# Turning P with plain matmuls into two banks, as row tiles where that suits, in a new order of work

## The chip, the cores and the metric

The kernel runs on one core of one Trainium2 chip. The metric is the time of one execution on the device in microseconds. Before the change it is 1505.74 us, the median of three runs (1505.22 to 1508.84).

The core has a matrix engine (TensorE, PE in the profile, with its weight loads shown apart as PEld), three engines for elementwise work (VectorE is DVE, ScalarE is ACT, GpSimd is POOL) and a queue that issues transfers (SyncE, SP). TensorE writes to PSUM, which has eight banks; DVE and ACT copy results out of it to SBUF ("eviction").

## What is computed

A sequence of 2048 rows of 448 numbers goes through four layers, each adding to x: attention with a recurrent memory (A), a gated network (B), A again, B again, with one set of weights for both A and one for both B.

```python
for s in range(n_seg):                      # 64 segments of 32 rows
    h = jnp.concatenate([mem, xs], axis=1)  # 8 memory rows and 32 of x: 40 keys
    q, k, v = (jnp.einsum('btd,dhe->bhte', h, W) for W in (Wq, Wk, Wv))  # 16 heads of 256
    scores = jnp.einsum('bhqe,bhke->bhqk', q, k) * scale   # masked
    p = _softmax(scores, axis=-1)
    o = jnp.einsum('bhqk,bhke->bhqe', p, v)
    o = jnp.einsum('bhte,hed->btd', o, Wo)
    mem = o[:, :M, :].copy()                # the next segment's memory
    outs.append(o[:, M:, :])
# B: gate = x W_gate; gate * (gate > 0) * (x W_up), times W_down
```

(The three projections stand in one line here for brevity.) Each A and B works on the layer-normalised x. All arrays are bf16. The memory makes a recurrence: segment s needs the memory of segment s-1.

## The kernel before

**Algebra.** The weights are multiplied together at the start: A = Wq Wk^T per head, so that scores are h A h^T, and B = Wv Wo per head, so that the output is the sum over heads of (P h) B. P is the softmax of one head's scores, h the 40 rows of a segment.

**Two streams of work.** The recurrence is `chain`, one step per segment. Both A layers run in it at once, the second seven segments (`LAG`) behind the first, in 70 steps. Per step: U = mem A for all heads (line 936, 112 matmuls), evicted and rearranged; then `middle`: scores (L1130), softmax on DVE and ACT, the turn of P, Y = P h (`y_part`, L1187 and L1190), evicted to YTm; then O, the 56 products with B (L975), evicted as a high and a low part (Ohi, Olo); then these are brought into columns with the selector `Sel` (`cols`, L451), which gives the next step's memory mT. In many steps `middle` runs a second time, for rows of x of the second layer that ride along with the memory rows through U and O; there are 66 such calls, with tiles Pr and PTr in place of Pm and PTm.

The rest is streaming: `att_group` does the 32 rows of four segments for four heads (U at L1276, scores at L1302, softmax, the turn of Px, Y at L1187 and L1190, output at L451), 96 groups in all; `glu_units` (L1374) and `glu_down` do the B layers, `norm` the normalisation with its own transposes. The streaming work fills TensorE between the steps of the recurrence.

**The turn of P.** Y = P h needs P with keys on the partitions, so P is transposed on TensorE and evicted to PT. In `middle`, P is one tile of 128 rows (16 heads by 8 memory rows) by 128 columns (two segments of 64, of which 40 are used); the turn is one 128x128 transpose in bf16 into one bank, and one copy of 104 rows by 128 columns to PTm or PTr. In `att_group`, Px holds four segments; its turn is two transposes into one bank and one copy of 104 by 256 to PTx. That makes 136 turns of one transpose and 96 of two.

**Tilings.** TensorE works untiled (128x128), as two row tiles (64x128: L1276, L1187, L1190, L1374), as four column tiles (128x32: L975), as eight tiles (64x32: L936) or as two column tiles (128x64, at the start). An operation's `mode` says which.

**What sets the order.** Every operation is recorded with `add`, with what it reads and writes, its engines and a cost, and `_Sched` lays out all engines' queues at build time. TensorE's order is written out: LINE holds a character per TensorE operation, which says how far down the list of those left the next one stands. ORDER gives a shift of priority to each part of the streaming work, which sets the order on the other engines. For each copy out of PSUM the planner picks ACT or DVE by its costs, and for each result a bank of the pools C (two banks) and G (six). An operation may be given further tilings in `also`; `line` cuts TensorE's order into runs whose operations have a tiling in common, and gives the run the lowest such mode. Where the planner foresees a long wait of TensorE it puts in matmuls without a use (L1408, "warming matmuls" below). Each engine works through its queue strictly in order and waits on semaphores.

Of the kernel before, what the change touches and what calls it, by code (L numbers as in the profile page):

```python
# [13 lines left out]
H = 16  # L14
E_HEAD = 256
NPAIR = H // 2
M = 8
# [10 lines left out]
BF = dt.bfloat16  # L28
# [1 line left out]


STEPS = "ABCDEFGHIJKLMNOPQRSTUVWXYZabcdefghijklmnopqrstuvwxyz0"
ORDER = ("WaAPMPvTtHAmiKXsPbQwBZAAKVLahkUWfxoglheAggVZZIjCfbeJAXlzkAApmXXSQGGARFrGGMUgYLYEqpMcimntsnbaLdDaYNUaIKQasootaa"
         "IamHzatMbanGYaAKt0aaJQPfHNWZggWPXLeJgyAiS0Lu0paxXy0bJaaawJabqAwkXQsLnJ0P0xdYLuR0IrxJESoh0aprYvAKeakBaTde0apmfl"
         "0AxKjloNZCHdAbpsDsUzAeRDrSYQfCauramiRROdJWQSliYOAntmwDkLvpaU0ose0NVHbcTnnAxX00lknAmXoAEI0JXsWoNrWtaR0aBTzbAueA"
         "zxZcQ0q0gag0TH0DuL0awknFmlrwNUBkrnZMushahJaOgAABbmsGORqpMzXeAbTAdCgmAA0qpoI0a00TKDzwtajkhAYHgKXubMoLxaAcZMeAky"
         "UPvecasMa0GlwBpnnaDqvPuaft0lUJZwIPBAtdSRexIzd0gdp0TFG0ZVaWtamLdLF0tecZgoaFmCnSxLrSAKbVEWWUbAUcbZAQKUWznAD0DwFY"
         "LhfiQS0H0vSOAAXZbJUSsFaria0uvIkcEZwBqzeVgvNgOaALCXLR0bnstXIDN0xuLBcRcqpzdacfaiZlTMhk0gMMHRwaBkgAisGZYtMsUFn0zV"
         "IFNwJApRZfcAiutYgwLmYo0w0xvGkIAceuiXs0DasLaajayO0oeyil0F0AqRaRioYDVAtQYbmvOVuSte0WMUqA0yKPaKRav0IjNTTO0lKZJvdk"
         "PxyqdoWnhLpAGweRybtOxXTBtFxgRZFGuwtA0XA0luZtjAvlcgOC0JAfaBWaBpTiUEtfuUcpuev0O0plQOMQhQAShmmAGTYotfgpbleII0TaBM"  # L40
         "aPnZY0dxoBWpVcrAiqamnnNot0unVPyLvpKpqAsABVrANdQWsSSKlz0JcSfj0ElEpn0qPKwWzaAgaYo00Aa0Tlb0oupJCA0yVSxuTnA0zokfbp"
         "CrqRqZjtboAdaHNayVAlkpQAMirRvHYYjqcposgwBwuwNAPImgFcnygdasArDIapCO00J0IZchpGLumthtqLsYG0apAkaPAtIR0rAB0uPdaaaa"
         "aacpbuKLoaaaaaaaaaaaaaaaaaaaOmqe0NbraUgWsbrP")

SIGNS = "ABCDEFGHIJKLMNOPQRSTUVWXYZabcdefghijklmnopqrstuvwxyz0123456789+-*/=<>()[]{}.,:;!"
LINE = ("AFFFEIFLJHFEFEFEJJEFGFHEEAEDMHHEDDEDEDDLKHDGDFDDDDKAJ,CEDEDCCCCKJAEGCEDBBMBBIACEBDCAAJALAHEnAADCCFGDEBAdcAWAMA"
        "AWnBAETkCSBBAHANNAgMBAKBWCAHAHGBbDAUDCAYBHBAAADPAENREAFLQHABQFPPFAFBDACCCCFBBABAAAWAAAKARBAHOdAGSAZAQAAABMS~DB"
        "A~BggA(AeCAAbAa9AZZZDADCAETADDQQAAAAMAAKKKAJJAIHAHGABEBACABAAAABATMAXAKVcLKAMRX~JXAMLA~NAAAEEADGAaaFFCCABETBBR"
        "WACPAANNNOAALAMvLA0DJCIHHLGGGGAFHHAADEKAACBBAEAAAABAMBAYXQAJGaIIAQAVAAAGDDAODDdcAFBBDDAAUaAACRAQBBNNNNAALAALL3"
        "3JKArIOICHBGGGAFIHeAEAEAACBBFAAAABCAATMBAXWeAJUaKJhMAW]AcKKAAAKEEATDA76fGmF2CABF4yBxAAAuuuCBbsAEpRFponEAAAjBLB"  # L50
        "glQAe9eeeECHcbTcbSBYBuFWBAATAARAJDSOOOAAMANLNMBdAbJDIAAPGUGZBgYBeEEEFHAGQDAvuCD~LCCqADAnNrm~BDCkkkFAAhDD;hhAAA"
        "cdjDACCYAAAVaAUATTTA0TBRDQQBBANAAAKCJBAHHHAKHGBBSGGAdcDEAZALQCBKZJBXBBBUIcJIFFBADGA))CEEon/H)CAB9jA7KD5556AA3H"
        "A32Ahzhy4FAAvAulCsssAiBEEonBFmmlDDATNCflCWABbJJEYsYYYCYXKXAWWAAITAAAAPODVNbNNNAALLEJAK+9YYDD5AA9E2FA0DIyyyzAOH"
        "vAvvBRsRBxqADACCAAjDAhDCFieeeAAcDJAaaxCCAXAAVAZAnSSssWARRRBABANAAZAACBAAGYSdlSSHGhZAFRAVAMDYABBeKBBBxHYBJEEB)("
        "HGDACOG+CA=B7ADe4CAG1112bAAyAAxxwdDkAzsbBFgoEnEmmmneFAEiENihFf-DeAGchABa2IZZZBCXAYIVXWEATDARCAAOfTBNUBMMMPBLEA"
        "L98DXeDVGIA0FAQAwFDTt~JDssstAZApArqDnANDCjAiEAmAfCCdAcccEAAZAYAAAWWAAAaTSvnARsRABBANNNAAMLAAXdAAAqBTGdASFFhPYF"
        "AQAACSBBgMBBBbIBQEBI{]ACSCC<FECCA+LEA7gD5556AA3A44bAiz70AZAxAwvluuuvAcsGHqqqGGAFtmFFFjIiBEAEeeeINEeAaAcbFBkEYA"
        "GATaAASRDHPVDOOOAANMA//ACIJA8=OOVH4Nc26BA000BAPyDwAvvNCSCAqEBAnNClCoAjjjEAiAgOC4CeeAAAbCAYBBAVqyVAAASSSASoACAA"
        "AMAAKYAdtkCJVIATISAGZgAFAAACNARMBeLdBBBFQFBADA))FCEoE/CAN>BE8B7AnCC333AGA0A21EYEexvAAVtb;rriBBArnnnCDmlQAkkPCB"
        "NAmfAAAcAaaBZZZCAYXFXHWWIAGADRXAAPANNEMMMEMVVNLEJRA77Ife4AHA16B0BAyyyAfCAuAtvuAsKAJpDAtHmAlBBKiiiEAAfAeCBddEAA"  # L60
        "DCXAWAAUZAAmStSSSASogAAAOBibxAvAZAAjYXgAJeYViYJJBnAASGAAARDC1cCJAZIBBBzIyIBEJEEBD77GFAnCIC0AB4BxB~NwAXuuu~GDtA"
        "VAtsGFADoAPsAljAjiANMfffAAdNAAdcBQYZAOBJUBLSBWRrGQQQRSDIDNDGNMLAFaJCAAGOATAEYEEEIFAACAAxwCMCTsABDBHnsAmMCBjjjA"
        "JAhCfAgfC}BAcDAAZYBXAAVVVWAATAVUsrSTAYuBRAAOOAAMMMAAKAYeAtkBWJBAIHkRbRFGSBdBEUEDOAMCCCGGCFIC{]ItU,(ADAA/BA-NB9"
        "99+AKA6CA65CdBA81bAAA3x3BwvmuuuActtsGtsHGGzpGGGmGApkjISAAfffEDdOcIeee;DaHbDYDejYfPWWeWWWXAAUNBBcbB/xQQYAdDAVDM"
        "TCARRRAACRPOKQQDGLCAAKIAAHAFFAEEEAACCABAWOVJHMARXFBAUAHAAGFAAALCCPDCDCFAJJFEBBBBBAABAADAAAAABAAAAA")


class _Op:
# [363 lines left out]
def mm_cost(*ns):  # L432
    return sum(max(n, 54) / 2.4 + 2.5 for n in ns)
# [14 lines left out]
def packed(E, mode, out, lhsT, rhs, **k):  # L448

    if mode != 1:  # L450
        return E.matmul(out, lhsT=lhsT, rhs=rhs, **k)  # L451
    for j in range(4):
        q = slice(32 * j, 32 * j + 32)
        w = lhsT[:, q] if len(lhsT.shape) == 2 else lhsT[:, j // 2, 32 * (j % 2):32 * (j % 2) + 32]
        i = E.matmul(out[q], lhsT=w, rhs=rhs, tile_position=(0, 32 * j), **k)
    return i


# [53 lines left out]
class _Kernel:  # L512
# [604 lines left out]
    def middle(self, act, m, row, col, P):  # L1117

        s = self.s
        k_ = lambda n: (m["n"], n)  # L1120
# [29 lines left out]
        else:  # L1150
# [7 lines left out]
            for c, sg, l in act:  # L1158
                b = sg % 2
                s.add("dve", 238, lambda E, e, c=c, b=b: E.tensor_scalar(Pv[:, b, 0:L], m["E"][:, c, 0:L], m["st"][:, 4 + c:5 + c], None, op0=ALU.mult),  # L1160
                      r=[k_("Em"), k_("rc")], w=[k_(f"P{c}")], **P)
# [8 lines left out]
        def yy(E, e):  # L1170
# [6 lines left out]
        s.add("pe", mm_cost(*[128] * 3, 64, 64), yy, r=[k_("PT")] + [q for c, sg, l in act for q in self.hr_keys(l, sg)], w=yb, alloc=yb, mode=2, **P)  # L1177
# [72 lines left out]
    def att_group(self, l, t, g, bo):  # L1250
# [65 lines left out]
        bp = self.bank("G", "C")  # L1316
# [6 lines left out]
        s.add("pe", mm_cost(128, 128), pt, r=[("Px", si), "ident"], w=[bp], alloc=[bp], room=["PTx"])  # L1323
        s.add(EV, ev_cost(256, fast=True), copy_any(PT[0:104, :], lambda: bp.ap().bitcast(BF)[0:104, 0:256]), r=[bp], w=["PTx"])

        for p in range(2):
            HR = self.HR[l][b][p]
            s.part()
            yb = [self.bank("G", "C") for _ in range(2)]

            def yy(E, e, p=p, HR=HR, yb=yb):
                for q in range(5):
                    for h in range(2):
                        r0 = 64 * h
                        i = self.y_part(E, yb[h].ap(), HR, r0, q, PT[r0:r0 + L, 128 * p:128 * p + 128], 128)
                return i
            hk = [q for h in range(2) for q in self.hr_keys(l, 4 * t + 2 * p + h)]
            s.add("pe", mm_cost(*[128] * 3, 64, 64), yy, r=["PTx"] + hk, w=yb, alloc=yb, room=[("YT", yi, p, h) for h in range(2)], mode=2)
# [194 lines left out]
```

## Time and profile before

| | |
|---|---|
| median of three runs | 1505.74 us |
| the profiled execution's own time | 1504.3 us |
| its span, first to last instruction | 1501.8 us |
| PE, DVE, ACT, POOL busy | 1487.6, 1148.6, 908.3, 171.8 us |
| matmuls | 37,022 |
| granted TensorE clock | 1.0 of full |

In the profile a row of a group has line, engine, operation, the output and inputs by name, their shapes, and the count; then busy time and the mean duration in ns, then the engine's idle time just ahead and what ended it. A row of the timeline has start and length in us, and merges equal instructions (x16) that follow each other; the durations of TensorE's instructions overlap, since they include the way through the array. Shapes such as 64\*128 are the tile of TensorE that a matmul uses, 64 rows by 128 columns. The lines named L441 and L444 are the shared copy function on ACT and DVE, and L451 the function `packed`, which many untiled matmuls go through, so that tiles' names tell them apart.

### The profile page before, as it was taken

The page shows a single profiled execution, that of the slowest core. Times are in us where ns is not written, and L with a number is a line of the kernel's source. Part 1 is how long each engine was busy: PE and PEld are TensorE (multiplying, and loading weights), DVE is VectorE, ACT ScalarE, POOL GpSimd, SP SyncE. Part 2 cuts the span into 40 slices and gives each one's busy share as a digit, 9 for nine tenths or more (in the row PEclk, how much of TensorE's full clock was granted, in tenths as well). Part 3 has the DMA queues.
Part 4 walks back from the last instruction along what each step waited for, and adds up shares of the span by engine and source line. Part 5 has one row for each costly group of instructions (what it writes and reads, how often), then busy time and mean ns, then how long its engine had stood idle before and what let it go on. Part 6 is the DMA issues. An engine that isn't in the chain of part 4 may idle for free.

```text
span 1501.8 us, 83238 instructions
## 1 busy us (share of the span) xinstructions
PE 1487.6 (99%) x37022; PEld 1057.6 (70%) x37022; DVE 1148.6 (76%) x3561; ACT 908.3 (60%) x2519; POOL 171.8 (11%) x664
## 2 busy tenths in 40 slices
PE   9999999999999999999999999999999999999999
PEld 6557666667767776777768677677768776677776
DVE  6667678787778878687877877687777788787864
ACT  7776566666556666566655666466665556565643
POOL 3110111111111111011100111011100011010000
PEclk9999999999999999999999999999999999999999
DMA  7612100000000000000000000000000000000000
GB/s 228 186 31 65 50 11 8 12 9 8 8 4 16 8 8 14 4 18 6 16 5 11 12 8 15 4 17 6 18 4 8 13 9 14 5 11 5 12 8 11
DMA packets 62581, 34.11 MB, mean 23 GB/s; under 512 B 31872, under 2 KB 62096, under 8 KB 62224
## 3 DMA queue, kind: packets, MB, share of 16 engines
q1 hardware_dynamic: 62224, 28.80, 7.5%
q8 instruction: 291, 4.77, 1.3%
q14 instruction: 66, 0.54, 0.1%
HBM read 21.36 MB, written 1.84 MB: 15 GB/s over the span
## 4 chain that ended last, share of the span: by engine, by line
PE 95%; DVE 3%; ACT 1%; SPq 0%; issue 0%; DMA 0%; POOL 0%; DVEq 0%
PE psG L451 24%; PE psG L1276 17%; PE psG L1374 12%; PE psC L975 11%; PE psC L936 9%; PE psG L936 3%; PE psG L1187 3%; PE psG L763 3%; PE psG L1302 3%; PE psC L451 2%; PE psC L1187 1%; PE psC L1130 1%; PE psG L750 1%; PE psG L1190 1%; PE psC L1276 1%; PE psG L975 1%
## 5 line engine op out<-in xcount | busy, mean ns | idle before, releaser
L1276 PE MATMUL psG<-HT,A 64*128 64x128 bf16 x4968 | 285.7, 216 | 0.2
L451 PE MATMUL psG<-Bsb,YT 128*128 128x448 bf16 x1288 | 276.6, 352 | 0.0
L1276 PE MATMUL psG<-HX,A 64*128 64x128 bf16 x3726 | 266.9, 216 | 0.2 <-issue 0.2
L1276 PEld LDWEIGHTS psG<-HT,A 64*128 64x128 bf16 x4968 | 234.2, 94 | 13.7 <-issue 5.4
L441 ACT ACTIVATE Ug<-psG 64x128 bf16<-64x128 f32 (+2 forms) x428 | 153.6, 378 | 68.3 <-PE psG L1276 59.4
L1276 PEld LDWEIGHTS psG<-HX,A 64*128 64x128 bf16 x3726 | 194.0, 94 | 1.0 <-issue 0.8
L1374 PE MATMUL psG<-G,glu 64*128 64x128 bf16 x5936 | 187.9, 216 | 0.6 <-DVE G L444 0.2
L1374 PEld LDWEIGHTS psG<-G,glu 64*128 64x128 bf16 x5936 | 174.2, 94 | 12.8 <-issue 6.3
L975 PE MATMUL psC<-Bsb,YTm 128*32 128x448 bf16 x3584 | 181.4, 353 | 1.0 <-DVE YTm L444 0.6
L451 PEld LDWEIGHTS psG<-Bsb,YT 128*128 128x128 bf16 x1288 | 112.5, 97 | 89.3 <-issue 5.9
L936 PE MATMUL psC<-A,mT 64*32 64x448 bf16 x3948 | 154.7, 350 | 1.5 <-DVE Pr L1160 0.5
L1114 DVE STREAM_TRANSPOSE uT<-Usb 128x384 bf16<-128x384 bf16 x280 | 154.1, 551 | 0.9
L936 PE MATMUL psG<-A,mT 64*32 64x448 bf16 x3892 | 152.1, 350 | 0.0
L975 PEld LDWEIGHTS psC<-Bsb,YTm 128*32 128x32 bf16 x3584 | 89.9, 97 | 73.4 <-DVE YTm L444 3.1
L441 ACT ACTIVATE YT<-psG 128x448 bf16<-128x448 f32 x238 | 120.6, 543 | 11.3 <-PE psG L1190 10.4
L444 DVE CAST Ug<-psG 64x128 bf16<-64x128 f32 (+2 forms) x274 | 112.8, 422 | 18.4 <-PE psG L1276 14.6
L936 PEld LDWEIGHTS psC<-A,mT 64*32 64x32 bf16 x3948 | 79.6, 92 | 58.1 <-ACT mT L441 5.9
L1379 ACT ACTIVATE hG<-psG 128x512 bf16<-128x512 f32 (+1 forms) x126 | 68.5, 544 | 65.6 <-PE psG L1374 61.6
L451 PE MATMUL psG<-glu,hG 128*128 128x448 bf16 x448 | 98.6, 352 | 0.0
L1380 DVE TENSOR_TENSOR hG<-hG,psG 128x512 bf16<-128x512 bf16 (+1 forms) x117 | 70.7, 610 | 32.5 <-ACT hG L1379 31.5
L981 ACT ACTIVATE Ohi<-psC 128x448 bf16<-128x448 f32 x66 | 35.9, 544 | 95.5 <-PE psC L975 94.2
L936 PEld LDWEIGHTS psG<-A,mT 64*32 64x32 bf16 x3892 | 79.8, 92 | 17.3 <-ACT mT L441 0.6
(242 smaller groups left out, 2889.4 us busy)
## 6 DMA issues: line engine op xcount, KB each, us to landing
HR<-xn SPq DMA_DIRECT2D x128, 32.0 KB
Tsb<-Rsb SPq DMA_DIRECT2D x256, 1.5 KB
Tsb<-Rsb SPq DMA_DIRECT2D x256, 2.0 KB
Bsb<-in_A_Wq_dram SPq DMA_DIRECT2D x6, 384.0 KB
Bsb<-in_A_Wk_dram SPq DMA_DIRECT2D x6, 384.0 KB
HR<-Rsb SPq DMA_DIRECT2D x126, 1.5 KB
HR<-Rsb SPq DMA_DIRECT2D x126, 2.0 KB
X<-in_A_x_dram SPq DMA_DIRECT2D x16, 112.0 KB
```

The lines of the kernel that those rows point to most:

```text
L441: return E.activation(out, i, ACT.Copy, scale=1.0 if scale is None else scale)
L444: return E.tensor_copy(out, i)
L451: return E.matmul(out, lhsT=lhsT, rhs=rhs, **k)
L763: i = E.matmul(bk.ap()[row0:row0 + mn, 0:D], lhsT=lhs[:, et, m0:m0 + mn], rhs=rhs[:, et, :], start=(et == 0), stop=(et == 1), tile_positio ...
L936: i = E.matmul(ub[v].ap()[32 * j:32 * j + 32, 0:D], lhsT=self.mT[rw, WHERE[b], first:first + 32], rhs=cols, start=(b == 0), stop=(b == 6), ...
L975: x = E.matmul(bo.ap()[32 * j:32 * j + 32, 0:D], lhsT=self.YTm[:, q, :], rhs=self.Bsb[:, chunks[q], :], start=(i == 0), stop=(i == 13), ti ...
L1114: self.s.add("dve", 578, lambda E, e, out=out, hh=hh: E.transpose(out, heads[hh]), r=[("Usb", 2 * half + v) for v in range(2)], w=[f"uT{ha ...
L1187: return E.matmul(ps[:, n * q:n * q + n], lhsT=HR[rows, 128 * q:128 * q + 128], rhs=PT, start=True, stop=True, tile_position=(b, 0))
L1276: i = E.matmul(ub[v].ap()[:, 128 * n:128 * n + 128], lhsT=self.A[rw, b, a0:a0 + 128], rhs=HT[rw, WHOLE[b], :, 0:SEG] if CROSS[b] is None e ...
L1374: i_ = E.matmul(two[v].ap()[:, 128 * c:128 * c + 128], lhsT=self.Wgu[rw, b, f0:f0 + 128], rhs=G[rw, WHOLE[b] if CROSS[b] is None else 4 + ...
L1379: s.add("act", 170 + 0.833 * N, lambda E, e, dst=dst, z=two[0], N=N: E.activation(dst, z.ap()[:, 0:N], ACT.Relu), r=[two[0]], w=[("hG", i, ...
L1380: s.add("dve", dv_cost(N), lambda E, e, z=two[1], N=N, dst=dst: E.tensor_tensor(dst, dst, z.ap()[:, 0:N], ALU.mult), r=[two[1]], w=[("hG", ...
```

## The change

The turn no longer uses the transpose operation. A new function `turned` multiplies P with columns of the identity: an f32 result, in two matmuls of 64 columns, one for each half of P's rows, each into a bank of its own. Untiled (mode 0), each of the two uses all 128 rows of P and half of the identity's columns. As row tiles (mode 2), each uses 64 rows of P and a 64x64 identity block, and the two lie on different rows of the array. `also=(2,)` leaves the choice to `line`. (The branch for mode 1 is not used by these calls.) The two banks are evicted one by one, so that each turn has two copies: of 64 columns in `middle`, of 128 columns in `att_group`. They are recorded under keys of their own, and the multiply that forms Y reads both. The `alloc` of a turn names two banks.

```diff
+def turned(E, mode, banks, at, P, ident):
+
+    for v in range(2):
+        rw = slice(64 * v, 64 * v + 64)
+        out = banks[v].ap()
+        if mode == 2:
+            i = E.matmul(out[:, at:at + 64], lhsT=P[rw, :], rhs=ident[rw, rw], start=True, stop=True, tile_position=(64 * v, 0))
...
+        else:
+            i = E.matmul(out[:, at:at + 64], lhsT=P, rhs=ident[:, rw], start=True, stop=True)
+    return i
...
-        bp = self.bank("C", "G")
-        s.add("pe", 56, lambda E, e: packed(E, e, bp.ap().bitcast(BF)[:, 0:128], m["P"][:, :], self.ident[:, :], is_transpose=True),
-              r=[k_("P"), k_("P0"), k_("P1"), "ident"], w=[bp], alloc=[bp], **P)
-        s.add(EV, ev_cost(128, fast=True), copy_any(m["PT"][0:104, :], lambda: bp.ap().bitcast(BF)[0:104, 0:128]), r=[bp], w=[k_("PT")], **P)
+        bp = [self.bank("C", "G") for _ in range(2)]
+        s.add("pe", 56, lambda E, e: turned(E, e, bp, 0, m["P"][:, :], self.ident),
+              r=[k_("P"), k_("P0"), k_("P1"), "ident"], w=bp, alloc=bp, also=(2,), **P)
+        for v in range(2):
+            s.add(EV, ev_cost(64), copy_any(m["PT"][0:104, 64 * v:64 * v + 64], lambda v=v: bp[v].ap()[0:104, 0:64]), r=[bp[v]], w=[k_(f"PT{v}")], **P)
...
-                i = packed(E, e, bp.ap().bitcast(BF)[:, 128 * p:128 * p + 128], Pf[:, 128 * p:128 * p + 128], self.ident[:, :], is_transpose=True)
+                i = turned(E, e, bp, 64 * p, Pf[:, 128 * p:128 * p + 128], self.ident)
...
-        s.add(EV, ev_cost(256, fast=True), copy_any(PT[0:104, :], lambda: bp.ap().bitcast(BF)[0:104, 0:256]), r=[bp], w=["PTx"])
+        for v in range(2):
+            s.add(EV, ev_cost(128), copy_any(PT[0:104, :].rearrange("p (a v q) -> p a v q", a=2, v=2)[:, :, v], lambda v=v: bp[v].ap()[0:104, 0:128].rearrange("p (a q) -> p a q", a=2)),
+                  r=[bp[v]], w=[("PTx", v)])
```

Beside this ORDER and LINE are replaced as a whole, so that all engines' queues differ in order from early on. In the changed program 70 of the 232 turns are row-tiled (38 of `att_group`, 32 of `middle`), 162 untiled.

More of the change, by code (lines that the diff above doesn't have):

```diff
@@ L32 @@
 STEPS = "ABCDEFGHIJKLMNOPQRSTUVWXYZabcdefghijklmnopqrstuvwxyz0"
[L33 to L43, printed above, removed]
@@ L455, in packed @@
         i = E.matmul(out[q], lhsT=w, rhs=rhs, tile_position=(0, 32 * j), **k)
+    return i
[5 more added lines that the diff above has]
+            i = E.matmul(out[:, at:at + 64], lhsT=P[rw, :], rhs=ident[rw, rw], start=True, stop=True, tile_position=(64 * v, 0))
+        elif mode == 1:
+            for j in range(4):
+                q = slice(32 * j, 32 * j + 32)
+                i = E.matmul(out[q, at:at + 64], lhsT=P[:, q], rhs=ident[:, rw], start=True, stop=True, tile_position=(0, 32 * j))
+        else:
+            i = E.matmul(out[:, at:at + 64], lhsT=P, rhs=ident[:, rw], start=True, stop=True)
     return i
@@ L1315, in att_group @@
         s.add("dve", dv_cost(160), lambda E, e: E.tensor_tensor(P[:, :, 0:L], T[:, :, :], bc(rc), ALU.mult), r=[k_("Tx"), k_("rc")], w=[("Px", si)])
-        bp = self.bank("G", "C")
+        bp = [self.bank("G", "C") for _ in range(2)]
         Pf = P[:, :, :].rearrange("p g k -> p (g k)")
@@ L1320, in pt @@
             for p in range(2):
[L1321 removed]
+                i = turned(E, e, bp, 64 * p, Pf[:, 128 * p:128 * p + 128], self.ident)
             return i
[L1323 to L1324 removed]
+        s.add("pe", mm_cost(128, 128), pt, r=[("Px", si), "ident"], w=bp, alloc=bp, room=["PTx", ("PTx", 0), ("PTx", 1)], also=(2,))
+        for v in range(2):
+            s.add(EV, ev_cost(128), copy_any(PT[0:104, :].rearrange("p (a v q) -> p a v q", a=2, v=2)[:, :, v], lambda v=v: bp[v].ap()[0:104, 0:128].rearrange("p (a q) -> p a q", a=2)),
+                  r=[bp[v]], w=[("PTx", v)])
         for p in range(2):
@@ L1337, in att_group @@
             hk = [q for h in range(2) for q in self.hr_keys(l, 4 * t + 2 * p + h)]
-            s.add("pe", mm_cost(*[128] * 3, 64, 64), yy, r=["PTx"] + hk, w=yb, alloc=yb, room=[("YT", yi, p, h) for h in range(2)], mode=2)
+            s.add("pe", mm_cost(*[128] * 3, 64, 64), yy, r=[("PTx", 0), ("PTx", 1)] + hk, w=yb, alloc=yb, room=[("YT", yi, p, h) for h in range(2)], mode=2)
             for h in range(2):
```

53 lines of the change are left out of this document (32 added, 21 removed).

## The prediction

> **What bounds the kernel now.** I read the page's busy times first, then its chain of work that ended last, then TensorE's waits, then the stretches of the span, and last TensorE's own instructions in order of time around some turns.
>
> ```profile
> PE 1487.6 (99%) x37022; PEld 1057.6 (70%) x37022; DVE 1148.6 (76%) x3561; ACT 908.3 (60%) x2519; POOL 171.8 (11%) x664
> PE 95%; DVE 3%; ACT 1%; SPq 0%; issue 0%; DMA 0%; POOL 0%; DVEq 0%
> ```
>
> TensorE (PE) is busy for 99% of the span and carries 95% of the chain. So the time is, nearly, the sum of what TensorE does; another engine counts only where TensorE has to wait for it. How often that is, the waits after the start (from 187 us on) and, of all waits of the span, the two for an evicted P tell:
>
> ```profile
> PE psC L975 <- DVE YTm L444: 0.6, 2, 0.3
> PE psC L451 <- DVE Olo L984: 0.6, 1, 0.6
> PE psC L936 <- DVE Pr L1160: 0.5, 1, 0.5
> ...
> PE psC L1187 <- ACT PTm L441: 0.4, 1, 0.4
> PE psC L1187 <- DVE PTm L444: 0.3, 1, 0.3
> ```
>
> Two of 232 turns (a turn: one P, or the two P tiles of a group, transposed and evicted) ended in a wait, 0.7 us together. The stretches show where TensorE is not full:
>
> ```profile
> 0.00:75.00 75.00, 71.50 (x980) 45.61 (x988) 50.21 (x116) 56.32 (x96) 15.72 (x51) 1.00 0.71 208
> 150.00:300.00 150.00, 145.75 (x3616) 98.00 (x3621) 112.61 (x357) 90.41 (x259) 18.58 (x75) 1.00 0.08 20
> 600.00:900.00 300.00, 299.48 (x7760) 218.37 (x7760) 234.46 (x737) 182.25 (x526) 33.14 (x130) 1.00 0.05 10
> ```
>
> (Length, then busy PE, PEld, DVE, ACT, POOL; then the granted clock.) From 600 to 900 us TensorE lacks 0.5 us of 300, from 0 to 75 and 150 to 300 it lacks 3.5 and 4.3. Past the start only less TensorE work makes the kernel faster, and nothing is left there for a better order to gain but the work itself.
>
> What the work costs must be read from start to start, since the durations overlap:
>
> ```profile
> 696.33 0.22 PE L1276 MATMUL psG<-HT,A 64*128 64x128 bf16 x2
> 696.48 0.23 PE L451 MATMUL psC<-ident,Pm 128*128 128x128 bf16 x1
> 696.65 1.12 PE L1374 MATMUL psG<-G,glu 64*128 64x128 bf16 x34
> ...
> 702.94 0.56 PE L1302 MATMUL psG<-HT,Ug 128*128 128x40 bf16 x16
> 703.34 0.92 PE L451 MATMUL psG<-glu,hG 128*128 128x448 bf16 x4
> 704.10 0.39 PE L451 MATMUL psG<-ident,xn 128*128 128x128 bf16 x4
> 704.32 0.92 PE L451 MATMUL psG<-glu,hG 128*128 128x448 bf16 x4
> ...
> 735.13 0.27 PE L451 MATMUL psG<-ident,Px 128*128 128x128 bf16 x2
> 735.34 0.23 PE L1187 MATMUL psC<-PTm,HR 40*128 40x128 bf16 x1
> ...
> 735.46 0.22 PE L1187 MATMUL psC<-PTm,HR 40*128 40x128 bf16 x1
> 735.47 0.22 PE L1187 MATMUL psG<-PTm,HR 40*128 40x128 bf16 x1
> 735.52 0.19 PE L1190 MATMUL psC<-PTm,HR 40*128 40x64 bf16 x1
> 735.52 0.19 PE L1190 MATMUL psG<-PTm,HR 40*128 40x64 bf16 x1
> 735.55 0.19 PE L1190 MATMUL psC<-PTm,HR 40*128 40x64 bf16 x1
> 735.55 0.19 PE L1190 MATMUL psG<-PTm,HR 40*128 40x64 bf16 x1
> 735.58 0.22 PE L1276 MATMUL psG<-HT,A 64*128 64x128 bf16 x2
> ```
>
> Five prices come from these starts. Four 128x128 transposes take 704.10 to 704.32: 0.055 us each, 56 ns unrounded. Sixteen untiled matmuls of 40 columns take 702.94 to 703.34: 25 ns each. Two row tiles (one per bank) of 128 columns start together and take 0.055 us as a pair (735.46 to 735.52), of 64 columns 0.03 us as a pair (735.52, 735.55, 735.58), 28 ns unrounded. Four of 448 columns take 0.76 us, 190 ns each. And a **change of tiling** costs about 95 ns: the last pair at 696.33 would be followed at 696.385 but the untiled turn starts at 696.48; the two turns at 735.13 need 0.112 and the tiled work after them starts 0.21 later.
>
> **The change part by part.** I counted the two programs' TensorE instructions in their order of issue; everything not named is equal in number.
>
> *Turns.* Before, 328 transposes (136 of Pm or Pr, 96 groups of two for Px) of 56 ns: 18.4 us. After, each is two matmuls of 64 columns. 220 stay untiled, 108 run as a pair of row tiles. A pair is priced by the 64-column pairs at 735.52: 108 x 28 ns = 3.0 us. No row has an untiled matmul of 64 columns; it lies between the 40-column one (25 ns) and the 128-column one (56 ns). I take 28 ns, half of the 56 for half of the columns, which is also what 64 columns cost at 735.52: 440 x 28 ns = 12.3 us. So the untiled turn costs what it did, and the tiled one half: 18.4 - 15.3 = **3.1 us less** (4.4 less at 25 ns, 9.2 more at 56 ns).
>
> *Changes of tiling.* From one matmul to the next the tile shape changes 619 times before and 576 times after. 43 x 95 ns = **4.1 us less**. This is the new order's and the tiled turns' doing together: of 232 turns 70 are now row-tiled and sit in tiled work.
>
> *Warming matmuls* that the kernel puts into foreseen waits: 28 short and 23 long before, 41 and 17 after, 5.9 us and 5.5 us by the prices above. They stand in place of idle time, so I count nothing (0.4 us less at the other end).
>
> *Evictions.* Each turn has two in place of one, 464 in place of 232. Their rows:
>
> ```profile
> L441 ACT ACTIVATE PTx<-psG 104x256 bf16<-104x256 bf16 x58 | 22.2, 383 | 13.1 <-PE psG L451 12.1
> L441 ACT ACTIVATE PTm<-psC 104x128 bf16<-104x128 bf16 x51 | 14.1, 277 | 40.0 <-PE psC L451 39.6
> L441 ACT ACTIVATE mC<-psC 128x128 bf16<-128x128 f32 x48 | 13.3, 277 | 1.6
> L441 ACT ACTIVATE mT<-psC 64x48 bf16<-64x48 f32 x52 | 10.5, 202 | 32.5 <-DVE mT L998 32.0
> L444 DVE COPY PTx<-psG 104x256 bf16<-104x256 bf16 x36 | 10.3, 285 | 12.3 <-PE psG L451 12.0
> L444 DVE CAST mC<-psC 128x128 bf16<-128x128 f32 x19 | 5.5, 292 | 0.7
> L998 DVE CAST mT<-psC 128x64 bf16<-128x64 f32 x67 | 14.8, 221 | 20.4 <-PE psC L451 20.4
> L444 DVE COPY PTm<-psC 104x128 bf16<-104x128 bf16 x15 | 3.3, 222 | 2.2 <-PE psC L451 2.2
> ```
>
> On ScalarE (ACT) 64 f32 columns lie between 202 ns (48) and 277 ns (128); in proportion about 217. 159 of them and 108 of 128 columns (277) replace 94 of 277 and 59 of 383: 64.4 - 48.6 = 16 us more. On VectorE (DVE) 113 of 221 and 84 of 292 replace 42 of 222 and 37 of 285: 49.5 - 19.9 = 30 us more. The two engines go to about 62% and 78%, so the extra work is hidden by idle time of theirs. What hides a turn's delay is TensorE's own work between the turn and the multiply that reads PT. By the prices above the median of it is 0.85 us before and 0.80 after in the recurrence, 1.8 and 1.5 in the groups, 2.0 and 1.5 in the riding steps. In the changed program's queues the two evictions stand on two engines in 111 of the 232 turns (then they end no later than the one did) and behind each other on one engine in 121, where the second ends some 0.16 us later (2 x 217 - 277) at most. With 0.8 us at hand I cost this at nothing; uncovered it is the rival below. The multiply waits for both, and everything behind it in TensorE's queue waits with it, the next step's U and O included.
>
> *Banks.* A turn holds two of the eight banks in place of one, for less than half a microsecond. Nothing in the waits shows TensorE short of banks; cost nothing, upper end in the second rival. GpSimd, SyncE and the transfers issue what they did, in another order; all DMA rows are the same in number.
>
> **Sum.** 3.1 + 4.1 = 7.2 us less. The profiled execution took 1504.3 us (span 1501.8), 1.4 under the median of the runs shown; against it the sum gives 1497.1, against the median 1505.7 - 7.2 = 1498.5.
>
> **A rule of the Trainium skill that speaks against it.** The load rows show each of the sixteen 40-column matmuls with a full 128x128 weight load of its own:
>
> ```profile
> 702.88 0.51 PEld L1302 LDWEIGHTS psG<-HT,Ug 128*128 128x128 bf16 x16
> ...
> L451 PEld LDWEIGHTS psG<-Bsb,YT 128*128 128x128 bf16 x1288 | 112.5, 97 | 89.3 <-issue 5.9
> ```
>
> Loads and matmuls of 25 ns spacing keep step, so a load of P does not hold back a 64-column matmul. The Trainium skill, page "TensorE: Matmul & The Clock Gate", sections "LDWEIGHTS (loading the stationary operand)" and "Back-to-back issue gap", says that a load takes its columns over 1.2 in ns (107 for 128 columns) and that pairs of load and matmul run at about 81 ns per matmul of 128 columns in a real kernel. By the 81 ns the 220 untiled turns would each cost one more load, 220 x 81 ns = 18 us more as an estimate, and the kernel would be slower. The trace does not agree (25 ns with a load each).
>
> **The rivals.**
> 1. *Evictions become the wait (slower).* The recurrence has 70 steps, each with one turn on its path. If in each step the second eviction came whole behind the first and nothing covered it, 70 x 217 ns = 15.2 us come back: 1498.5 + 15.2 = 1513.7. It makes the kernel slower than the 0.3% (4.5 us, about what a measurement of this kernel can tell) from 11.7 us on, 0.167 us in each step. For it: 121 turns have both evictions on one engine, DVE is at 76% before. Against: 0.7 us of waits for PT in all, and unchanged cover. "TensorEngine Tiling (Array Packing)" in the Trainium skill, section "PSUM Bottleneck", warns of just this, that eviction does not get faster with the tiles; no run here shows it yet.
> 2. *The start eats it (no change).* The stretches above lack 3.5 us and 4.3 us in the loading and filling stage, where TensorE waits for transfers and evictions, banks among them. The new order changes this stage too. Another 5 us of such waits, about half as much again, gives 1503.5.
> 3. *Loads bound the small matmuls (slower).* If each untiled matmul of a turn waited out one load of 97 ns, as the second load row has it, in place of 28: 440 x 69 ns = 30 us, 1529. The row of sixteen is against it.
> 4. *The row tiles do not overlap.* Then a tiled turn costs 56 ns again, 3.0 us are lost: 1501.5. The pairs at 735.52 are against it.
>
> **How the numbers follow.** Forecast 0.66, rivals 0.11, 0.17, 0.03 and 0.03. The forecast's own range is 1494 to 1501: 1.3 us from the 25 ns, 0.4 from the warming matmuls, and 3 us either way for waits that fall otherwise in another order. The whole range goes up to the middle of rivals 1 and 2: 1494 to 1506, which leaves out rival 3, most of rival 1 and a little at the low end. Faster is the forecast and a share of rival 4: 0.67; same is rival 2 and the rest of rival 4: 0.19; slower is rivals 1 and 3: 0.14.
>
> **What would show it.** Starts of the untiled 64-column matmuls 28 ns apart (right) or 56 and more (wrong); the two row tiles of a turn starting together; some 576 changes of 95 ns; TensorE's waits for PTm, PTr and PTx still about 1 us (right) or 10 (rival 1); the two first stretches lacking 8 us (right) or 13 (rival 2). ACT and DVE should be busier by 16 and 30 us without the span noticing. The prediction is wrong if TensorE's work shrinks by 7 us and the idle time grows by as much.

## The result: 2.6 us faster, of 7.2 forecast

The changed kernel takes 1502.49 us (median of 20 runs, 1499.49 to 1506.63), the kernel before 1505.08 us in the same comparison (20 runs, 1504.04 to 1508.84). The ratio is 0.998, with an interval of 0.9974 to 0.9986. Two later comparisons, each against runs of the kernel before on the same chip, gave 3.6 and 3.75 us. So the change makes the kernel some 3 us faster, about half of the forecast 7.2 or less, though inside its range of 1494 to 1506.

### The profile after

The profiled execution has a span of 1499.7 us, 2.1 less than before. From its page come the busy times, the chain of work that ended last by engine, and the packets, megabytes and share of the queue that brings the engines their instructions:

```profile
PE 1482.7 (99%) x37357; PEld 1058.9 (71%) x37357; DVE 1157.8 (77%) x3670; ACT 916.3 (61%) x2643; POOL 169.9 (11%) x663
q8 instruction: 294, 4.82, 1.4%
PE 94%; DVE 3%; ACT 1%; issue 1%; SPq 1%; DMA 0%; POOL 0%; DVEq 0%; POOLq 0%
```

TensorE (PE) issues 335 matmuls more and is busy for 4.9 us less. In the chain, PE went from 95% to 94%, and "issue", which is time in which an engine waited for nothing that the profile shows, from 0% to 1% (6.4 us before, 11.2 now, added up). The stretches (length, then busy PE, PEld, DVE, ACT, POOL, then the granted clock):

```profile
0.00:75.00 75.00, 71.00 (x963) 45.40 (x971) 51.11 (x119) 53.89 (x91) 15.50 (x51) 1.00 0.72 208
150.00:300.00 150.00, 145.93 (x3669) 98.98 (x3675) 112.77 (x367) 91.26 (x271) 19.64 (x78) 1.00 0.08 21
600.00:900.00 300.00, 299.62 (x7855) 219.24 (x7855) 238.03 (x764) 182.45 (x551) 32.70 (x131) 1.00 0.05 11
```

In the first two TensorE lacks 4.0 and 4.1 us, 8.1 together against 7.8 before, in the third 0.4 against 0.5. TensorE's waits from 187 us on, by line, what was waited for, us in total, times, longest:

```profile
PE psG L1293 <- issue: 1.5, 5, 0.4
PE psG L952 <- issue: 0.9, 1, 0.9
PE psG L451 <- DVE Olo L1000: 0.7, 2, 0.4
PE psG L1204 <- DVE PTm L444: 0.5, 2, 0.4
...
PE psG L1204 <- ACT PTm L441: 0.2, 1, 0.2
```

The largest are two that wait for no engine. Before, the list had only waits for DVE, ACT and POOL at its top. The waits for an evicted P are as small as they were: 0.7 us before, and 0.7 here.

Two pieces of TensorE's timeline (start, length) show the turn itself, untiled and row-tiled:

```profile
664.84 0.28 PE L471 MATMUL psG<-ident,Px 128*128 128x64 bf16 x4
664.95 0.54 PE L451 MATMUL psG<-Bsb,YT 128*128 128x448 bf16 x2
...
1045.81 0.22 PE L465 MATMUL psG<-ident,Px 64*128 64x64 bf16 x4
1045.86 0.22 PE L1393 MATMUL psG<-G,glu 64*128 64x128 bf16 x1
```

Four untiled matmuls of 64 columns occupy 664.84 to 664.95; over all such neighbours the mean from start to start is 29.4 ns (median 29). Four row-tiled ones are recorded from one start, and the next work begins 0.05 us later: two pairs, and a pair takes no longer than one of its tiles would. The two evictions of a turn:

```profile
L441 ACT ACTIVATE PTx<-psG 104x128 bf16<-104x128 f32 x106 | 26.2, 275 | 12.7 <-PE psG L471 11.7 <-PE psC L471 0.3
L441 ACT ACTIVATE PTm<-psC 104x64 bf16<-104x64 f32 x70 | 14.0, 221 | 32.7 <-PE psC L471 26.9 <-PE psG L471 5.8
L444 DVE CAST PTx<-psG 104x128 bf16<-104x128 f32 x79 | 21.1, 283 | 8.3 <-PE psG L471 6.1 <-PE psG L465 2.0
L444 DVE CAST PTm<-psC 104x64 bf16<-104x64 f32 x47 | 10.1, 221 | 8.8 <-PE psC L471 7.7 <-PE psG L465 0.5 <-PE psC L465 0.5
```

The prices are those that were taken (275, 221, 283 and 221 ns against 277, 217, 292 and 221).

### Where the rest of the 7 us is

The page can't answer that by a single row, so I worked out four sums from the start times of TensorE's matmuls, in the same way for each kernel. **Work** is every matmul at the start-to-start price of its shape (those of the prediction, 29.4 ns for the untiled 64 columns) and 95 ns for each change of tiling. **Pauses inside** are gaps of over 80 ns beyond that price in the middle of an operation, where no semaphore stands and nothing can be waited for. **Late waits** are gaps at the start of an operation after 320 us, and **early waits** those before. The sums are mine and no rows. Means over two profiled executions of the kernel before and four of the changed one (one of these with an irrelevant edit, told below), in us:

| | before | after | difference |
|---|---|---|---|
| span | 1502.6 | 1498.9 | -3.7 |
| work | 1458.7 | 1451.8 | -6.9 |
| pauses inside operations | 3.0 (2.5, 3.5) | 5.4 (4.6 to 6.0) | +2.4 |
| late waits | 2.2 | 3.3 | +1.1 |
| early waits | 14.3 | 13.6 | -0.7 |

The four sums leave 24.4 and 24.8 us of the spans unsorted, gaps of under 80 ns among them. The work shrank by nearly what was forecast. About half of it came back, most of that in pauses in which TensorE waits for no engine and no transfer of data. With two and four executions the growth of the pauses is a small sample, but the two ranges do not touch.

What such a pause looks like, in the timeline of the changed kernel, at two places (in brackets the idle time that the profile puts before the instruction):

```profile
817.65 0.22 PE L1293 MATMUL psG<-HX,A 64*128 64x128 bf16 x1
...
818.16 0.21 PE L1293 MATMUL psG<-HX,A 64*128 64x128 bf16 x1 [0.30 <-issue]
818.17 0.15 PEld L1293 LDWEIGHTS psG<-HT,A 64*128 64x128 bf16 x4 [0.47 <-issue]
```

```profile
1243.37 0.22 PE L1293 MATMUL psG<-HT,A 64*128 64x128 bf16 x1
1244.02 0.21 PE L1293 MATMUL psG<-HT,A 64*128 64x128 bf16 x1 [0.43 <-issue]
```

In the midst of one operation's row-tiled matmuls, whose pairs start 0.055 us apart, the next start comes after 0.51 and 0.65 us. Weight loads stop too (the PEld row). The transfers of the 4 us around the second pause, from 1240.4 to 1244.4, in forty slices of 0.1 us (GB/s), and the queue of instructions in the same window:

```profile
GB/s 0 0 0 0 0 0 0 0 0 0 164 0 0 0 0 0 0 0 0 14 0 1 1 0 0 0 0 0 0 0 6 10 0 0 0 0 0 0 21 0
q8 instruction: 1, 0.02, 1.6%
```

One packet of 16 KB moves, in the slice at 1241.4 us. By the packets' records it has landed at 1242.43, and the pause ends 1.6 us after that. This holds for nearly all: the pauses of this execution and of that before end 1.3 to 1.6 us after such a packet has landed, but for one at 225.8 us (2.5 us after), while packets come only every 5 us (294 in the span).

### The profile page after: what moved, and what is told of

Same layout as the page of the kernel before. It is cut to its first block, busy times and chain, and to the rows that moved or that the text cites. A ratio compares the mean times of both kernels' runs of the same rounds, so it can differ in the third digit from the quotient of the medians.

```text
span 1499.7 us, 84217 instructions
## 1 busy us (share of the span) xinstructions
PE 1482.7 (99%) x37357; PEld 1058.9 (71%) x37357; DVE 1157.8 (77%) x3670; ACT 916.3 (61%) x2643; POOL 169.9 (11%) x663
## 4 chain that ended last, share of the span: by engine, by line
PE 94%; DVE 3%; ACT 1%; issue 1%; SPq 1%; DMA 0%; POOL 0%; DVEq 0%; POOLq 0%
PE psG L451 23%; PE psG L1293 17%; PE psG L1393 11%; PE psC L991 10%; PE psC L952 9%; PE psG L952 4%; PE psG L1204 3%; PE psG L779 3%; PE psG L1319 2%; PE psG L991 2%; PE psC L451 1%; PE psC L1146 1%; PE psC L1204 1%; PE psG L766 1%; PE psG L1207 1%; PE psC L1293 1%
## 5 line engine op out<-in xcount | busy, mean ns | idle before, releaser
L451 PE MATMUL psG<-Bsb,YT 128*128 128x448 bf16 x1344 | 285.9, 352 | 0.0
L451 PEld LDWEIGHTS psG<-Bsb,YT 128*128 128x128 bf16 x1344 | 116.6, 97 | 98.5 <-issue 8.9
L1393 PEld LDWEIGHTS psG<-G,glu 64*128 64x128 bf16 x5726 | 169.7, 94 | 9.4 <-issue 4.7
L991 PE MATMUL psC<-Bsb,YTm 128*32 128x448 bf16 x3192 | 161.9, 353 | 0.7 <-DVE Tr L1168 0.3
L952 PE MATMUL psG<-A,mT 64*32 64x448 bf16 x4116 | 157.0, 350 | 1.3 <-issue 0.9
L952 PE MATMUL psC<-A,mT 64*32 64x448 bf16 x3724 | 147.7, 350 | 0.7 <-ACT mT L441 0.5
L444 DVE CAST Ug<-psG 128x256 bf16<-128x256 f32 (+2 forms) x281 | 113.8, 416 | 17.1 <-PE psG L1293 11.8
L991 PEld LDWEIGHTS psC<-Bsb,YTm 128*32 128x32 bf16 x3192 | 80.5, 97 | 62.8 <-issue 1.3
L451 PE MATMUL psG<-glu,hG 128*128 128x448 bf16 x420 | 93.4, 352 | 0.1
L444 DVE CAST YT<-psG 128x448 bf16<-128x448 f32 x128 | 77.6, 616 | 11.9 <-PE psG L1207 11.2
```

What stands on the lines that cost most here:

```text
L444: return E.tensor_copy(out, i)
L952: i = E.matmul(ub[v].ap()[32 * j:32 * j + 32, 0:D], lhsT=self.mT[rw, WHERE[b], first:first + 32], rhs=cols, start=(b == 0), stop=(b == 6), ...
L991: x = E.matmul(bo.ap()[32 * j:32 * j + 32, 0:D], lhsT=self.YTm[:, q, :], rhs=self.Bsb[:, chunks[q], :], start=(i == 0), stop=(i == 13), ti ...
L1393: i_ = E.matmul(two[v].ap()[:, 128 * c:128 * c + 128], lhsT=self.Wgu[rw, b, f0:f0 + 128], rhs=G[rw, WHOLE[b] if CROSS[b] is None else 4 + ...
```

## The experiments

Each kernel was compared with the kernel before in runs on the same chip, whose median differs a little by chip (1503.06 to 1504.97); differences are against that. All kernels here compute the whole result.

### Do the turn and the order each bring their part?

The changed turn under the old ORDER and LINE:

```diff
-ORDER = ("KXAPMPBMRaALECWggYQTnrAFAEp...
+ORDER = ("WaAPMPvTtHAmiKXsPbQwBZAAKVL...
-LINE = ("AGFEEMEJGFGEEGEENLEGEGGFEEEM...
+LINE = ("AFFFEIFLJHFEFEFEJJEFGFHEEAED...
```

> The changed turn (two banks, two evictions, row tiles allowed) under the ORDER and LINE of before. Counted: 613 changes of tiling (before 619), 44 turns row-tiled, 334 matmuls more; TensorE's work by the prices of the prediction (29 ns for the untiled 64-column matmul) is within 0.5 us of before. Theory A (the gain is eaten by pauses of TensorE inside its operations, which no semaphore explains and which follow the landing of a block of its instructions; evictions cost nothing): 1505 +- 2 us. Theory B (the doubled evictions make TensorE wait): 3 to 6 us slower than before, with more waits for PTm, PTr and PTx.

Measured: 1513.71 us against 1503.63, 10.1 us **slower** (ratio 1.0069, 1.0057 to 1.0081), more than either theory expected. And the old turn under the new ORDER and LINE (the same edit the other way round, on the kernel before):

> The old turn (one transpose each, one bank, one eviction) under the new ORDER and LINE. Counted: 656 changes of tiling, 37 more than before and 80 more than after: at 95 ns each TensorE's work is about 4 to 5 us more than before. Both theories: about 1509 to 1511 us; if the new order alone brought the gain it would be 1502.

Measured: 1512.13 us, 8.5 us slower (1.0059, 1.0047 to 1.0071). Neither part stands alone. The new order with the old turn changes tiling 656 times, since the places that it gives to turns suit row tiles; its work is 5.0 us more than before. The new turn in the old places finds only 35 that suit row tiles (44 pairs of matmuls; the expectation calls these 44 turns), changes tiling 613 times and has the same work as before (+0.1), but its late waits are 9.3 us in place of 2.2. The chain of this kernel, and waits of its TensorE:

```profile
PE 90%; DVE 5%; ACT 3%; issue 1%; SPq 1%; DMA 0%; POOL 0%; DVEq 0%
```

```profile
PE psG L465 <- ACT YTm L441: 0.7, 1, 0.7
PE psG L1319 <- ACT Ug L441: 0.6, 2, 0.4
```

ACT and DVE carry 8% of the chain, twice what they did. These largest waits after the start are not for an evicted P. L465 is the turn itself, held up by a copy of YTm, which it needs nothing of but the bank; L1319, the scores, waits for a copy of its own input.

### What do the row tiles bring?

The changed kernel without the choice of row tiles, all turns untiled:

```diff
-              r=[k_("P"), k_("P0"), k_("P1"), "ident"], w=bp, alloc=bp, also=(2,), **P)
+              r=[k_("P"), k_("P0"), k_("P1"), "ident"], w=bp, alloc=bp, **P)
```

(and the same in `att_group`)

> The change with its turns left untiled throughout (no second tiling allowed), new order. Counted: 655 changes of tiling, 79 more than after, and 108 pairs of matmuls in sequence in place of side by side. By the prices 79 x 95 ns + 108 x 30 ns = 10.7 us more work than after: 1513 us under theory A. Beside order_old_turn it differs in the doubled evictions and some 320 matmuls at equal work: theory A expects it 1 to 3 us slower than that one (the two 64-column matmuls cost 59 ns and not 56, and more instructions), theory B 4 us or more.

Measured: 1510.93 us, 7.3 slower than before (1.0055, 1.0042 to 1.0067) and 11 slower than the changed kernel. There are 655 changes of tiling, and by my sums 11.0 us more work than in the changed kernel: 79 changes of 95 ns are 7.5 us, 108 pairs as untiled matmuls 3.3. So in the new order the gain of the change lies in the 70 row-tiled turns, as the prediction priced them.

The changed kernel, in which only these 70 keep the new turn and the 162 untiled ones go back to one transpose, one bank and one copy, as in the kernel before (the list of which turns are tiled is written out):

```diff
+        if TILED[self.ti - 1] == ".":
+            bp = self.bank("C", "G")
+            s.add("pe", 56, lambda E, e: packed(E, e, bp.ap().bitcast(BF)[:, 0:128], m["P"][:, :], self.ident[:, :], is_transpose=True),
+                  r=[k_("P"), k_("P0"), k_("P1"), "ident"], w=[bp], alloc=[bp], **P)
+            s.add(EV, ev_cost(128, fast=True), copy_any(m["PT"][0:104, :], lambda: bp.ap().bitcast(BF)[0:104, 0:128]), r=[bp], w=[k_("PT0"), k_("PT1")], **P)
+        else:
...
```

> As after, but the 162 turns that run untiled use the old transpose, one bank and one eviction; the 70 row-tiled turns stay. 578 changes of tiling, 214 matmuls fewer than after, 162 evictions fewer. Theory A: TensorE's work within 1 us of after, fewer instructions, so 1501 to 1503 us, the pauses falling otherwise. Theory B: the waits of the doubled evictions go and most of the missing 4.6 us comes back: 1498 to 1499 us.

Measured: 1499.42 us, 4.2 us faster than before (0.9975, 0.9965 to 0.9984). Since that seemed to beat the changed kernel, both were run again on one chip:

> The changed kernel a third time, as the measure for the other three on the same chip: 2.5 to 4 us under before.

> mixed once more: 3.5 to 5 us under before. If the untiled turns' extra matmuls, banks and evictions are what the new order has left unpaid, it is 1 us or more under after_third; if the new order has absorbed them, the two are equal within 0.5 us.

Measured: 1501.22 (0.9979, 0.997 to 0.9988) and 1501.57 us (0.9981, 0.9972 to 0.9989). They are equal. This version has 0.7 us more work and 1.9 us more late waits, but only 1.3 and 2.1 us of pauses inside operations, against 4.6 to 6.0: most of the pauses are gone, and other waits take up what that gains. So the additions of the 162 untiled turns (214 matmuls, a second copy and bank each) cost the changed kernel no time that these runs can tell.

### What is a pause?

If TensorE's instructions come too late, then more instructions without any work must make it worse. To the kernel before I added three waits ahead of each of TensorE's operations past the hundredth, for a count that was reached long ago: 2935 instructions that do nothing, at an operation's start.

```diff
-            for o, waits, inc in plans[eng]:
+            for n, (o, waits, inc) in enumerate(plans[eng]):
+                if eng == "pe" and n > 100:
+                    for _ in range(3):
+                        E.wait_ge(sems["act"], 1)
```

> The kernel before with its work, order and evictions unchanged; ahead of each TensorE operation past the hundredth stand waits that are long fulfilled, 2935 instructions more on TensorE's queue (4%, 11 or 12 blocks of 16 KB more). Theory A (TensorE runs out of instructions where small matmuls follow each other densely): the pauses inside operations, 3.5 us in the profiled run of before, grow to 8 us or more, and the kernel is slower by as much, 1508 to 1515 us. Theory B (only evictions make TensorE wait): no change, 1503 to 1505 us.

Measured: 1566.57 us against 1503.38, **63 us slower** (1.0419, 1.0402 to 1.0436), five times the most that was expected. From its page, the chain and the queue of instructions:

```profile
PE 93%; DVE 2%; issue 2%; ACT 2%; SPq 1%; DMA 0%; POOL 0%; DVEq 0%
q8 instruction: 303, 4.96, 1.3%
```

The waits from 187 us on, and the stretch of the span that lacked 0.5 us before:

```profile
PE psG L1279 <- issue: 4.6, 12, 1.0
PE psG L939 <- issue: 3.0, 5, 0.8
PE psC L939 <- issue: 2.9, 5, 1.0
PE psG L1377 <- issue: 1.8, 4, 0.6
```

```profile
600.00:900.00 300.00, 293.76 (x7390) 210.84 (x7378) 230.26 (x727) 177.25 (x513) 30.88 (x123) 1.00 0.04 10
```

Twelve packets more come (303 against 291 before), 245 added instructions to a packet. Pauses inside operations, where none of the added waits stands, rise from 3.5 to 31 us in 65 places, and the four largest waits are for "issue". So instructions that carry no work slow TensorE down at places far from themselves. What it does not separate is how much of the other half of the 63 us the added waits cost at the operations' starts (late waits rose to 20 us, early ones to 21).

The other question is whether the pauses sit at certain places of the program. Two kernels: the changed one unaltered, and the same with 17 warming matmuls of 448 columns at the start cut into 68 of 112, so that all that follows lies 102 instructions (51 matmuls with their loads) further on in the queue:

```diff
-            for _ in range(17):
-                i = E.matmul(wb.ap()[:, 0:D], lhsT=hG[:, 0:128], rhs=hG[:, 128:576], start=True, stop=True)
+            for _ in range(68):
+                i = E.matmul(wb.ap()[:, 0:112], lhsT=hG[:, 0:128], rhs=hG[:, 128:240], start=True, stop=True)
```

> The changed kernel once more, as a second sample of its pauses and as the measure for after_shift on the same chip: 1498 to 1503 us, 2 to 5 us under before; pauses inside operations of 3 to 8 us if they depend on the moment at which a block lands, the same 6 us at the same places if they belong to the program alone.

> The changed kernel with its 17 warming matmuls of 448 columns at the very start cut into 68 of 112 columns: the same columns, 102 instructions more ahead of all others, so every later instruction lies 102 places further in its 16 KB block of 256. Theory A: the pauses inside operations fall at other places and add up to another sum (between 1 and 9 us; after: 6), the time moving with them. Theory B: no change of time or of where TensorE pauses, within 1 us of after_again.

Measured: 1499.79 (0.9977, 0.9968 to 0.9987) and 1499.81 us (0.9974, 0.9964 to 0.9985), both 3.6 faster than before. The pauses keep to a place in the queue, not in the program. Count the records of TensorE's queue (loads, matmuls and waits) from the first: the changed kernel has 75,456, some 256 for each of its 294 packets. Then every pause inside an operation from 50 us on, some 240 in the 18 profiled executions of this document, comes at the 193rd, 194th or 195th record of 256. That holds with the shift too, where the program stands 102 records further on. So a pause is the passage from one packet's block of instructions to the next. (This count takes gaps of over 80 ns beyond the usual distance of two such matmuls; its sums differ from those of the table by up to 1 us.)

Which of the passages pause is in part the same each time: of 27 that did so in three executions of the changed kernel, 11 did in two or three of them, that near 1005 us in all three (1005.5, 1004.1 and 1005.8); that at 910.4 us did so only once. The sums are alike with the shift and without (4.6 against 6.0 and 5.3), and the time is the same.

### How much of it do the turn's own additions cause?

The turn adds matmuls, copies and a held bank. Each was put alone into the kernel before, in the old order. First the copies: each eviction cut into two of half the columns, from one bank, the multiply waiting for both.

```diff
-        s.add(EV, ev_cost(128, fast=True), copy_any(m["PT"][0:104, :], lambda: bp.ap().bitcast(BF)[0:104, 0:128]), r=[bp], w=[k_("PT")], **P)
+        for v in range(2):
+            s.add(EV, ev_cost(64), copy_any(m["PT"][0:104, 64 * v:64 * v + 64], lambda v=v: bp.ap().bitcast(BF)[0:104, 64 * v:64 * v + 64]), r=[bp], w=[k_(f"PT{v}")], **P)
```

(and so in `att_group`)

> The kernel before with its transposes, its one bank for each turn and its order; only the eviction of each turn is cut in two, 464 copies in place of 232. Counted: 621 changes of tiling, TensorE's work within 1 us. If the waits of turn_old_order (8 us more on evictions) come from the number of evictions, this one is slower by 4 to 8 us too (1508 to 1512); if they come from the second bank, it is within 2 us of before.

Measured: 1507.06 us, 3.7 us slower (1.0025, 1.0016 to 1.0034). Next the bank: a second one taken with each turn, unused, until its eviction is done.

```diff
-        bp = self.bank("C", "G")
+        bp, b2 = self.bank("C", "G"), self.bank("C", "G")
...
-              r=[k_("P"), k_("P0"), k_("P1"), "ident"], w=[bp], alloc=[bp], **P)
+              r=[k_("P"), k_("P0"), k_("P1"), "ident"], w=[bp, b2], alloc=[bp, b2], **P)
...
```

> The kernel before in everything, only that each turn also takes a second bank, unused, until its eviction is done. If the part of turn_old_order's loss that split does not show (6 of 10 us) comes from holding two banks, this one is 3 to 6 us slower than before; if banks are free, as the prediction has it, it is within 1.5 us.

Measured: 1508.23 us, 5.2 us slower (1.0036, 1.0024 to 1.0049); late waits are 5.7 us where the kernel before has 2.2. The third is the number of matmuls. One plain matmul of 128 columns with an f32 result in place of the transpose, and the same cut into two of 64 columns into the same bank, with one eviction, so that the two kernels differ in 328 matmuls and nothing else:

```diff
-            for v in range(1):
-                i = E.matmul(bp.ap()[:, 128 * v:128 * v + 128], lhsT=m["P"][:, :], rhs=self.ident[:, 128 * v:128 * v + 128], start=True, stop=True)
+            for v in range(2):
+                i = E.matmul(bp.ap()[:, 64 * v:64 * v + 64], lhsT=m["P"][:, :], rhs=self.ident[:, 64 * v:64 * v + 64], start=True, stop=True)
```

> The kernel before with its order, one bank and one eviction for each turn, the transpose replaced by one plain matmul of 128 columns (f32 in PSUM). It is the measure for halves. Copies of f32 cost DVE 292 in place of 222 ns and about 416 in place of 285: both theories 1503 to 1507 us.

> As whole, but each matmul of a turn is cut into two of 64 columns into the same bank: 328 matmuls and as many weight loads more, evictions, banks, order and queues of the other engines the same. By 29.4 ns for 64 columns the work is 328 x 2.8 ns = 0.9 us more. Theory A (instruction supply): 1 to 4 us slower than whole, the rest over 0.9 in pauses inside operations. Theory B (evictions alone): 0.9 us slower than whole.

Measured: 1503.99 (1.0009, 1.0 to 1.0018) and 1506.50 us (1.0026, 1.0016 to 1.0035), a difference of 2.5 us, known to about 1 us. Only 0.9 us of it is streaming (328 x 2 x 29.4 - 328 x 56 ns). Their chains, whole and then halved:

```profile
PE 94%; DVE 3%; ACT 1%; SPq 0%; issue 0%; DMA 0%; POOL 0%; DVEq 0%
```

```profile
PE 94%; DVE 3%; ACT 1%; issue 1%; SPq 0%; DMA 0%; POOL 0%; DVEq 0%
```

The "issue" time of the chain goes from 6.4 to 7.8 us. The same pair in the new order, in the 162 untiled turns alone (220 matmuls more):

> mixed with the 162 untiled turns as one plain matmul of 128 columns in place of a transpose, one bank, one eviction (f32): the measure for mixed_halves, 0 to 2 us over mixed_again (whole was 0.9 over before).

> mixed_whole with each of those matmuls cut into two of 64 columns into the same bank: 220 matmuls more, 0.6 us of work, nothing else. If the instruction supply is what the new order has not absorbed: 1.5 to 3 us over mixed_whole (old order: 2.5 for 328). If it has: 0.6 us.

Measured: 1502.83 (0.9984, 0.9975 to 0.9993) and 1504.87 us (1.0004, 0.9995 to 1.0012), a difference of 2.0 us, known to about 1.5 us, of which 0.6 is streaming. The pauses inside go from 4.6 to 7.1 us, though the "issue" time of the chain does not follow (11.6 and 10.8 us). The largest wait for "issue" of either, the whole one first:

```profile
PE psG L1308 <- issue: 0.5, 1, 0.5
```

```profile
PE psG L1421 <- issue: 2.2, 6, 0.6
```

So about 1.5 us lie in the number of matmuls itself, in either order, beyond what they stream. In the old order the copies, the bank, the f32 result and the added matmuls make 3.7 + 5.2 + 0.9 + 2.5 = 12.3 us; taking off some 1.8 for its 44 row-tiled pairs and 6 fewer changes of tiling leaves 10.5. The whole turn in that order was measured at 10.1; with each term known to about 1 us, so close a match is partly luck. One more look at the kernel before, for a second set of sums:

> The kernel before once more, as a second sample of its pauses: 2 to 5 us inside operations (3.5 in the first profiled run, 6.0 and 5.3 in the two of after) if the difference of 2 us between the kernels is theirs and not chance; 5 to 7 us if it is chance.

Measured: 1505.23 us, span 1503.4, pauses 2.5 us in 10 places. It stands in the table above.

What did not fit: the kernel with whole untiled turns has as many matmuls as the one with transposes, and yet 4.6 us of pauses against 1.3 and 2.1; in the old order it is the other way (1.2 against 2.5 and 3.5). By the count over all traces, the changed turn in the old order has 3.0 us of pauses and the kernel with untiled turns throughout 3.4, each with as many matmuls as the changed kernel, which has 3.9 to 5.8; the kernel before has 2.2 and 2.9. So the count of instructions alone does not decide on them. What else does stays open, as does why a packet is late at one time and not at another.

## Why the prediction was wrong in size

**The step that failed** is the first, on what bounds the kernel: "the time is, nearly, the sum of what TensorE does; another engine counts only where TensorE has to wait for it", and "nothing is left there for a better order to gain but the work itself". It left a third state out: TensorE neither working nor waiting for an engine, but without instructions. It was there to be seen, in 3 us of pauses inside operations before the change, yet the sum has no term for it, nor for waits that the new order might add. In the changed kernel 2.4 us of the 6.9 that were won went into such pauses, at the passages between blocks of instructions, and 1.1 into late waits. That the added matmuls are what made the pauses grow is not shown for this kernel: in the two pairs that differ by nothing else they cost 1.4 to 1.6 us beyond their streaming, but leaving 214 of them out of the changed kernel brought no time that these runs can tell. Why its pauses grew stays open.

**Changes of tiling** (4.1 us): right. There are 576, and work fell as they say. That the gain is the order's and the tiles' together is shown from both sides: the order alone costs 8.5 us, the order without row tiles 7.3.

**Turns** (3.1 us): right for row tiles (two pairs in 0.05 us), 0.6 us too good for the untiled ones (440 x 1.4 ns), which take 29.4 ns and not 28. The work fell by 6.9 = 3.1 - 0.6 + 4.1 + 0.4, the last for the warming matmuls counted at nothing, within rounding.

**Evictions and banks** (nothing): right in this kernel, where waits for PT stay at 0.7 us, late waits grow by about 1, and the version with 162 turns on one copy and one bank is as fast, but not for the reason that was given. The cover named was TensorE's work between turn and multiply and idle time on ACT and DVE. In the old order, where that cover is no smaller, the copies cost 3.7 us and the banks 5.2. They are nearly free in the new order, which came with them; what in that order hides them no run shows. The turn's copies take 59.4 and 46.3 us on ACT and DVE, 10.9 and 26.5 more; the totals of these engines rose by only 8.0 and 9.2, where 16 and 30 were forecast. I did not follow the rest of that difference.

**Rival 1** (evictions become the wait, 1513.7) did not happen here. The changed turn in the old order comes out at that time, 1513.71, by chance: the loss there is a sum of copies, banks and matmuls, and TensorE's largest waits are for other results than PT. The Trainium skill, page "TensorEngine Tiling (Array Packing)", sections "PSUM Bottleneck" and "Gotcha 1: PSUM Pressure", names both causes: eviction doesn't get faster with tiles, and row tiles need several banks. The runs agree for the old order, where the second copy and the second bank cost 3.7 and 5.2 us for 232 turns, not for the new.

**Rival 2** (the start eats it) forecast about the loss that came, at the wrong place. The two first stretches lack 8.1 us against 7.8, and early waits did not grow.

**Rival 3** (loads bound the small matmuls) is refuted: 29.4 ns for 64 columns with a load each. The Trainium skill gives 81 ns per matmul of 128 columns with its load, on the page "TensorE: Matmul & The Clock Gate", section "Back-to-back issue gap"; the trace does not agree, with 56 ns for 128 columns before the change and 29.4 ns for 64 after. **Rival 4** (the tiles don't overlap) is refuted by the rows at 1045.81.

The prediction's own last sentence said what would make it wrong: work smaller by 7 us and idle time larger by as much. It went almost half that way. One reading in the prediction is off without consequence: the middle of rivals 1 and 2, which it gives as the upper end of its range, is 1508.6 and not 1506.

## What to carry to other kernels

When a kernel's bounding engine is at 99%, look for pauses in the midst of its operations before forecasting a gain: an edit that replaces one instruction by several shorter ones can leave the work nearly alone and still lose time to the supply of instructions. The chain's "issue" entry is only a hint of it: one version here has 9.7 us of it with 1.3 us of pauses. Price a part that is "hidden" in the order in which it will run, since the same two copies and second bank cost 9 us in the old order and about 1 us of late waits in the new one. A change of code and a new order have to be taken apart by running both halves, since here each half alone was slower than the kernel before.

## What was unexpected of the hardware

- TensorE stops in the middle of an operation, with no semaphore to wait for, for 0.1 to 1.2 us, 10 to 16 times in an execution of the kernel before or the changed one, always at the passage from one block of 256 instructions to the next, and mostly until 1.3 to 1.6 us after a 16 KB packet of the instruction queue has landed. Of the passages that pause, some do so in each execution of a program and most in one alone.
- 2935 waits that had long been fulfilled, 3 ahead of an operation, cost 63 us, some 21 ns each, and 28 us of that show up inside operations.
- An untiled matmul of 64 columns with its own 128x128 weight load takes 29.4 ns, and 328 matmuls cut in two cost 7.6 ns per added matmul, of which 2.8 are streaming.
- To hold a second bank, unused, for each of 232 turns costs 5.2 us, 22 ns a turn, though no wait in the trace of before shows TensorE short of banks.
